# Packed queries, keys and queries of the first batches turned by TensorE; the second batch's expert chosen early; opening buffers and loads re-ordered

## The chip, the cores and the metric

One core of one Trainium2 chip runs the whole program. The metric is device time in microseconds, the median of several executions of the same program; smaller is better. TensorE multiplies matrices into eight PSUM banks, VectorE (DVE), ScalarE (ACT) and GpSimd (POOL) work on what it leaves, and SyncE (SP) issues nearly all DMA loads and stores, in the order of its program.

## What is computed

Shapes: 8 batches, 8 heads, 576 tokens, 64 values per head (model width 512), 32 packed queries per head, 8 experts with hidden width 1024. All data is float32.

```
p_packed = softmax(p @ k.T / 8) @ v           # 32 packed rows per batch and head
a        = softmax(q @ p_packed.T / 8) @ p_packed
x        = a with the heads side by side      # [8, 576, 512]
logits   = x @ w_gate ;  local = sigmoid(x @ w_local)
for each batch b, token s in order:
    fresh = argmax(logits[b, s])
    e     = fresh if s == 0 or local[b, s] < 0.5 else the expert of token s - 1
    out[b, s] = softmax(logits[b, s])[e] * (relu(x[b, s] @ w1[e]) @ w2[e])
```

## The kernel before

The kernel takes one expert per batch, that of token 0, and does all 576 tokens of the batch with it; a block behind the main program (L1170 on) repeats the batch for other experts if some token strayed. A batch's attention is done for two "quads" Q of four heads. Per quad: `scores` (L485) multiplies packed queries and keys, `keys` (L520 to L576) does the softmax, the product with v and turns the result to `ppT`; `queries` (L605) multiplies q with it, and `soften` (L642 to L668) turns the result to the softmax weights `a2t`, split into a rounded part `a2h` and a remainder `a2l`. x is never built: `pack_weights` (L932; in the first batch `pack_quarters`, L903) multiplies w1 with `ppT`, and `layer1` (L972) multiplies that with `a2h` and `a2l`. Each product is done as three (high times high, high times low, low times high), which is what the splits `wph`/`wpl` and `w2s` (L958, L960) are for. `layer2` (L1000, L1005, L1009) multiplies with w2 in 8 chunks, in two passes over the tokens ("half" 0 and 1).

**Who is turned where.** Scores need packed queries and keys with the 64 values on the partitions. In the first batch p was loaded four times (32 rows each, side by side on the partitions) and turned by DVE in blocks of 32 (L401), the keys too (L446, L448), so its score matmuls had 32 rows, and four DVE reductions per quad (L495) followed. Batch 1's keys and the queries of batches 0 and 1 were turned by TensorE in blocks of 128 (`turn_tokens`, L415 and L423, copied by ACT at L417 and L425); later batches are loaded in small blocks and turned by DVE (L439, L589).

**Who chooses the expert when.** `gates` (L759 to L843) takes logits of all tokens from the finished `a2t`. For the first batch alone, `early_choice` (L715 to L747) works out the logits of token 0 from its query (`q0`) and `ppT`; it holds one PSUM bank from its start to its choice. `choose` writes the expert's number, SP reads it into a register (`ereg`), and the loads of w1 (L869, L882) and w2 (L856) follow.

**What sets the order.** The program's order is made when it is built. Every step is a generator that yields conditions (`need`: tiles written, buffer slots and PSUM banks free, a condition `when`). `weave` (from L1133) takes the next step that is ready by a model of times (`Clock`), loads first, then side work of the earliest batch, then the main chunks; `soon` is the first batch without `ereg`, and later batches' side work waits for idle engines. Where the model sees TensorE wait, before the first chunks, it puts in matmuls on a constant tile (`keep_warm`, L214), one for each FILL ns. w1 and w2 of the first batch are loaded in the order `FIRST` ("1" a quarter of w1, "2" a chunk of w2, "v" the values of batch 1). Buffers per tag are in `BUFS`; `w2raw` has 4, `w2s` 8, `w1t` 2.

## Time and profile before

| what | value |
|---|---|
| median of 3 runs | 435.56 us (434.97 to 435.76) |
| profiled execution | 436.44 us, span 434.7 us |
| granted TensorE clock, mean | 0.987 |
| busy: TensorE, DVE, ACT, POOL | 416.2, 296.2, 177.6, 36.8 us |
| matmuls on the constant tile (L214) | 146 records, 22.2 us |
| one load of w1 (quarter), w2 (chunk), v (quad) | 512, 256, 512 KB |
| HBM read, written | 63.07 MB, 9.44 MB |

Busy shares are means over stages with different limits, so they are read stage by stage below. A float32 matmul leaves two records in the trace. A record's duration includes its way through the array, and matmuls overlap, so the duration of a group of them is the time that counts. L numbers are lines of the kernel before.

### The profile page before, as it was taken

The page shows a single profiled execution, that of the slowest core. Times are in us where ns is not written, and L with a number is a line of the kernel's source. Part 1 is how long each engine was busy: PE and PEld are TensorE (multiplying, and loading weights), DVE is VectorE, ACT ScalarE, POOL GpSimd, SP SyncE. Part 2 cuts the span into 40 slices and gives each one's busy share as a digit, 9 for nine tenths or more (in the row PEclk, how much of TensorE's full clock was granted, in tenths as well). Part 3 has the DMA queues.
Part 4 walks back from the last instruction along what each step waited for, and adds up shares of the span by engine and source line. Part 5 has one row for each costly group of instructions (what it writes and reads, how often), then busy time and mean ns, then how long its engine had stood idle before and what let it go on. Part 6 is the DMA issues. An engine that isn't in the chain of part 4 may idle for free.

```text
span 434.7 us, 10230 instructions
## 1 busy us (share of the span) xinstructions
PE 416.2 (96%) x3935; PEld 333.1 (77%) x3936; DVE 296.2 (68%) x862; ACT 177.6 (41%) x413; POOL 36.8 (8%) x56
## 2 busy tenths in 40 slices
PE   8899999959999999999999999999999999999994
PEld 8777787816887788786887588878887678878883
DVE  3576858677787588768967697829977588637221
ACT  1264743317342543435443462345433543345221
POOL 2001520200030000200020003000020000200000
PEclk9999999959999999999999999999999999999999
DMA  7879798074999379973999679983999340464011
GB/s 212 250 210 339 198 135 144 4 288 152 179 127 274 110 235 148 166 287 99 198 129 194 224 211 152 156 316 121 201 135 260 125 146 0 131 230 138 0 62 56
DMA packets 163024, 73.25 MB, mean 169 GB/s; under 512 B 127896, under 2 KB 143000, under 8 KB 162968
## 3 DMA queue, kind: packets, MB, share of 16 engines
q1 hardware_dynamic: 161720, 72.11, 74.7%
q8 instruction: 33, 0.54, 0.6%
q10 hardware_dynamic: 1248, 0.41, 0.4%
q14 instruction: 23, 0.19, 0.1%
HBM read 63.07 MB, written 9.44 MB: 167 GB/s over the span
## 4 chain that ended last, share of the span: by engine, by line
PE 80%; DVE 9%; DMA 4%; issue 3%; ACT 1%; SPq 1%; POOLq 0%; POOL 0%; DVEq 0%; ACTq 0%
PE bank L1000 36%; PE bank L972 20%; PE bank L1005 3%; PE bank L1009 3%; PE bank L214 3%; DMA w1t<-in_moe_w_dram 3%; PE bank L554 2%; PE bank L932 2%; PE bank L485 2%; PE bank L529 2%; DVE qn L589 2%; PE bank L605 2%; DMA qn<-in_q_dram 1%; DVE wpl L946 1%; DVE h L987 1%
## 5 line engine op out<-in xcount | busy, mean ns | idle before, releaser
L1000 PE MATMUL bank<-w2s,h 128*128 128x512 f32 x768 | 205.2, 399 | 2.3 <-DVE w2s L960 1.1
L1000 PEld LDWEIGHTS bank<-w2s,h 128*128 128x128 f32 x768 | 135.8, 188 | 32.7 <-issue 4.8
L987 DVE SCALAR_TENSOR_TENSOR h<-bank,h 128x256 fp32r<-128x256 f32 x192 | 61.1, 345 | 64.1 <-ACT h L983 63.9
L983 ACT ACTIVATE h<-bank 128x256 fp32r<-128x256 f32 (+1 forms) x128 | 52.9, 413 | 111.6 <-PE bank L972 107.0
L972 PEld LDWEIGHTS bank<-a2h,wph 128*128 128x128 f32 x256 | 47.0, 188 | 16.9 <-ACT wph L943 3.3
L972 PE MATMUL bank<-a2h,wph 128*128 128x320 f32 (+1 forms) x256 | 57.0, 304 | 0.0
L972 PE MATMUL bank<-a2h,wpl 128*128 128x320 f32 (+1 forms) x256 | 55.8, 297 | 1.0 <-DVE wpl L946 0.9
L972 PE MATMUL bank<-a2l,wph 128*128 128x320 f32 (+1 forms) x256 | 54.6, 294 | 0.0
L668 POOL TENSOR_TENSOR a2l<-a2t,a2h 128x576 fp32r<-128x576 f32 (+2 forms) x17 | 23.3, 1373 | 300.7 <-ACT a2h L665 300.7
L972 PEld LDWEIGHTS bank<-a2h,wpl 128*128 128x128 f32 x256 | 40.9, 188 | 2.0 <-DVE wpl L946 2.0
L972 PEld LDWEIGHTS bank<-a2l,wph 128*128 128x128 f32 x256 | 41.1, 188 | 0.0
L960 DVE TENSOR_TENSOR w2s<-w2raw,w2s 128x512 fp32r<-128x512 f32 x58 | 38.5, 693 | 0.6 <-ACT w2s L958 0.6
L958 ACT CAST w2s<-w2raw 128x512 fp32r<-128x512 f32 x64 | 38.0, 623 | 1.6 <-DMA w2raw<-in_moe_w_dram 1.4
L1005 PE MATMUL bank<-w2s,h 128*128 128x512 f32 x64 | 26.0, 406 | 0.0
L1009 PE MATMUL bank<-w2s,h 128*64 128x512 f32 x64 | 25.2, 394 | 0.0
L946 DVE TENSOR_TENSOR wpl<-bank,wph 128x512 fp32r<-128x512 f32 x28 | 18.1, 680 | 7.9 <-ACT wph L943 7.9
L214 PE MATMUL bank<-warm 128*128 128x128 f32 x146 | 22.2, 307 | 1.1 <-DVE warm L209 1.1
L214 PEld LDWEIGHTS bank<-warm 128*128 128x128 f32 x146 | 20.5, 219 | 1.8 <-issue 0.9
L520 ACT ACTIVATE a<-a,nb 128x576 f32<-128x576 f32 x16 | 12.4, 777 | 22.1 <-DVE nb L506 22.1
L943 ACT CAST wph<-bank 128x512 fp32r<-128x512 f32 x28 | 14.9, 599 | 11.8 <-PE bank L932 11.7
L625 DVE STREAM_TRANSPOSE sT<-bank 128x288 f32<-128x288 f32 (+2 forms) x36 | 13.2, 418 | 8.1 <-ACT gate L623 8.1
L495 DVE TENSOR_SCALAR_CACHE_REDUCE a<-bank 128x288 f32<-128x288 f32 (+2 forms) x36 | 13.6, 419 | 5.4 <-PE bank L485 5.1
(142 smaller groups left out, 445.2 us busy)
## 6 DMA issues: line engine op xcount, KB each, us to landing
w2raw<-in_moe_w_dram SPq DMA_DIRECT2D x64, 256.0 KB, 6.2
w1t<-in_moe_w_dram SPq DMA_DIRECT2D x14, 1024.0 KB, 6.1
kv<-in_v_dram SPq DMA_DIRECT2D x16, 512.0 KB, 6.1
out_dram<-o SPq DMA_DIRECT2D x31, 256.0 KB, 2.1
qn<-in_k_dram SPq DMA_DIRECT2D x24, 288.0 KB, 7.3
qn<-in_q_dram SPq DMA_DIRECT2D x24, 288.0 KB, 6.9
kv<-in_q_dram SPq DMA_DIRECT2D x4, 512.0 KB, 6.6
w1t<-in_moe_w_dram SPq DMA_DIRECT2D x4, 512.0 KB, 5.5
```

What stands on the lines that cost most here:

```text
L214: nc.tensor.matmul(out=warm_ps[:, :128], lhsT=warm, rhs=warm, start=True, stop=True)
L668: eng.tensor_tensor(out=a2l, in0=a2t, in1=a2h.bitcast(F32), op=ALU.subtract)
L943: nc.scalar.copy(out=hi[fh][:, Q], in_=ts[fh, Q])
L946: nc.vector.tensor_tensor(out=lo[fh][:, Q], in0=ts[fh, Q], in1=hi[fh][:, Q].bitcast(F32), op=ALU.subtract)
L958: nc.scalar.copy(out=w[:, 0], in_=raw)
L960: (nc.gpsimd if st["early"] and c > 1 else nc.vector).tensor_tensor(out=w[:, 1], in0=raw, in1=w[:, 0].bitcast(F32), op=ALU.subtract)
L972: nc.tensor.matmul(out=t[:, :GROUP * (m1 - m0)], lhsT=st["wp"][c // 4][wi][:, Q, fs], rhs=a2[ai][Q][:, GROUP * m0:GROUP * m1], start=(n == ...
L983: nc.scalar.activation(out=h[:, :w], in_=t[:, :w], func=AF.Relu)
L987: nc.vector.scalar_tensor_tensor(out=h[:, dst:dst + z - a], in0=t[:, a:z], scalar=0.0, in1=h[:, a:z].bitcast(F32), op0=ALU.max, op1=ALU.su ...
L1000: nc.tensor.matmul(out=acc, lhsT=hs[hi], rhs=w[:, wi], start=(c == 0 and n == 0), stop=(c == NC - 1 and n == 2),)
L1005: nc.tensor.matmul(out=acc, lhsT=h[:, 256:WIDE + TAIL], rhs=w[:, 0], start=(c == 0), stop=False, skip_group_check=True,)
L1009: nc.tensor.matmul(out=acc[0:TAIL], lhsT=h[:, 256:WIDE], rhs=w[:, 1], start=False, stop=(c == NC - 1), skip_group_check=True,)
```

## The change

Packed queries are loaded once, 128 rows (four heads by 32) by two groups, twice side by side on the free axis, and turned by two TensorE transposes and one ACT copy; this holds for batches 0 and 1. Batch 0's keys go the way of batch 1's: `turn_tokens`. Its score matmuls have 64 rows, so two reductions per quad follow. Keys and queries of the first two batches are loaded into other slots (`w2s`, `kv`, and `o` for the last 64 tokens). Batch 1 gets `early_choice` and `gate_weights`, with a second `q0`. Its queries are loaded from `FIRST`, behind the first w1 pieces, and its remainders of w2 are subtracted by POOL. The constant matmuls are bf16 of 512 columns instead of float32 of 128; the model doubles TensorE's times up to 6500 ns and starts it at 3700 instead of 5400. `soon` and some conditions ask for `settled` (expert known and softmax done) instead of `ereg`.

```
-WARM, FILL = 10, 240.0
+WARM, FILL = 6, 230.0
-START, FIRST_LOAD = 5400.0, 700.0
+START, FIRST_LOAD, COLD = 3700.0, 700.0, 6500.0
-FIRST = "1 2 1 2 2 v 1 2 1 2 2 2 2".split()
+FIRST = "1 2 1 2 2 q 1 2 v 1 2 2 2 2".split()
...
+            full *= 2.0 if self.engine("PE") < COLD else 1.0
...
-            nc.tensor.matmul(out=warm_ps[:, :128], lhsT=warm, rhs=warm, start=True, stop=True)
+            nc.tensor.matmul(out=warm_ps, lhsT=heat[:, :128], rhs=heat, start=True, stop=True)
...
+    def settled(b):
+        return "ereg" in sts[b] and sts[b]["quads"] == [NQ, NQ]
...
     def load_packs(b, queues):
-        x = tile_([128, H, D], F32, "p_in")
-        clock.rate = 150.0
+        x = tile_([128, 2, 2 * D], F32, "p_in")
+        clock.rate = 400.0
         for z, queue in enumerate(queues):
-            queue.dma_start(out=x[NP * z:NP * z + NP], in_=at(p, b).rearrange("h n d -> n h d"))
+            queue.dma_start(out=x[:, :, D * z:D * z + D], in_=at(p, b).rearrange("(g h) n d -> (h n) g d", g=2))
...
-            st["p"] = load_packs(b, (nc.sync, nc.scalar, nc.sync, nc.scalar))
+            st["px"] = load_packs(b, (nc.sync, nc.scalar))
...
-            order = (("k", 0), ("k", 1), ("q", 0), ("q", 1), ("p", 1)) if st["second"] else \
+            order = (("k", 0), ("k", 1), ("p", 1)) if st["second"] else \
...
+            if name == "q" and isinstance(b, int) and b == 2:
+                yield need(when=lambda: len(sts[1].get("w1", ())) == 2)
...
     def turn_packs(st):
-        yield need(when=lambda: "p" in st)
-        yield need(st["p"])
-        turn(st["p"])
-        st["pT"] = st["p"].rearrange("a h (x n) -> a h x n", n=NP)
+        yield need(when=lambda: "px" in st)
+        yield need(st["px"], slot="pT", banks=1, by=("Activation",))
+        tp = bank()
+        for g in range(2):
+            nc.tensor.transpose(out=tp[:, 128 * g:128 * g + 128], in_=st["px"][:, g], identity=ident)
+        give(st["px"])
+        yield need(tp, by=("Activation",))
+        st["p"] = st["pT"] = tile_([128, H * NP], F32, "pT")
+        nc.scalar.copy(out=st["pT"], in_=tp[:, 0:H * NP])
+        give(tp)
...
-                nc.scalar.copy(
+                (nc.vector.tensor_copy if early and Q == 0 and n else nc.scalar.copy)(
...
-        if part is None:
+        if part is None and not st["pairs"]:
...
-            if not st["early"]:
+            if not st["pairs"]:
                 yield from choose(st, cd[0:1, 0:1])
...
-                        yield need(slot="kv")
-                        sts[1]["v", Q] = load_values(1, Q)
+                        yield need(slot="kv" if kind == "v" else ("kv", "o"))
+                        sts[1][kind, Q] = load_values(1, Q) if kind == "v" else load_pairs(sts[1], kind, Q)
...
-            (nc.gpsimd if st["early"] and c > 1 else nc.vector).tensor_tensor(
+            (nc.gpsimd if st["second"] or st["early"] and c > 1 else nc.vector).tensor_tensor(
...
-                    *((turn_packs(st), early_choice(st), turn_small()) if early else ()),
-                    *((turn_tokens(st, "k"), turn_keys(st, 0)) if started == 1 else (turn_keys(st, Q) for Q in both)),
+                    *((turn_small(),) if early else ()), *((early_choice(st),) if started < 2 else ()),
+                    *((turn_packs(st), turn_tokens(st, "k")) if started < 2 else (turn_keys(st, Q) for Q in both)),
...
-            soon = next((b for b in range(B) if "ereg" not in sts[b]), B) if at_batch[0] >= 0 else 0
+            soon = next((b for b in range(B) if not settled(b)), B) if at_batch[0] >= 0 else 0
```

## Rows read from the trace of the kernel before

**Rows 1.** Stretches: us; busy us of PE, PEld, DVE, ACT, POOL; clock, DMA, GB/s.

```profile
1.00:7.00 6.00, 5.90 (x27) 5.91 (x28) 2.87 (x8) 1.28 (x1) 2.00 (x11) 1.00 0.76 203
34.50:43.20 8.70, 7.79 (x75) 6.11 (x74) 5.74 (x16) 2.89 (x8) 1.29 (x1) 1.00 1.10 335
43.20:86.60 43.40, 43.37 (x458) 34.61 (x458) 30.41 (x108) 20.50 (x53) 11.81 (x13) 1.00 0.71 122
86.60:99.45 12.85, 7.47 (x70) 2.13 (x70) 9.14 (x29) 3.02 (x7) 0.00 (x0) 0.60 0.68 246
99.45:426.00 326.55, 322.73 (x2839) 260.26 (x2831) 231.14 (x634) 136.79 (x312) 20.30 (x24) 1.00 0.77 163
```

**Rows 2.** Chain of waits in order of time: start, us, what.

```profile
1.10 8.45 PE bank L214 x48
...
10.73 2.43 PE bank L214 x20
...
35.42 7.68 DMA w1t<-in_moe_w_dram
```

**Rows 3.** Timeline of the opening: start, us, engine, line, operation.

```profile
6.24 0.43 DVE L448 STREAM_TRANSPOSE kf<-kf 64x256 f32<-64x256 f32 x1
...
9.48 1.12 PE L485 MATMUL bank<-kf,p_in 32*32 32x160 f32 x64
...
11.60 1.23 DVE L446 STREAM_TRANSPOSE kf<-kf 128x1024 f32<-128x1024 f32 x1
...
22.09 0.27 ACT L576 COPY ppT<-bank 128x128 f32<-128x128 f32 x1 [2.03 <-PE bank L575]
...
34.53 0.54 PE L972 MATMUL bank<-a2h,wph 128*128 128x320 f32 x2
```

**Rows 4.** Timeline of SP's queue, 20 to 140 us: issues of loads.

```profile
27.72 0.42 SPq L869 DMA_DIRECT2D w1t<-in_moe_w_dram  x1
...
38.62 8.53 SPq L856 DMA_DIRECT2D w2raw<-in_moe_w_dram  x4
...
52.45 7.93 SPq L336 DMA_DIRECT2D qn<-in_k_dram  x4
...
85.56 1.08 SPq L882 DMA_DIRECT2D w1t<-in_moe_w_dram  x2
```

**Rows 5.** Timeline of PE: w1 packed for batch 1 and for batch 2.

```profile
96.04 3.48 PE L932 MATMUL bank<-w1t,ppT 64*32 64x512 f32 x32
...
143.88 1.95 PE L932 MATMUL bank<-w1t,ppT 64*32 64x512 f32 x32
```

**Rows 6.** Timeline of PE and DVE: prices of single steps.

```profile
10.49 0.32 DVE L495 TENSOR_SCALAR_CACHE_REDUCE a<-bank 128x160 f32<-128x160 f32 x1 [3.82 <-PE bank L485]
...
19.42 0.27 PE L715 MATMUL bank<-q,ppT 64*32 64x32 f32 x8
...
21.18 0.66 PE L415 MATMUL bank<-ident,kv 128*128 128x128 f32 x4
...
46.32 1.20 PE L485 MATMUL bank<-qn,p_in 64*32 64x288 f32 x32
...
47.07 0.46 DVE L495 TENSOR_SCALAR_CACHE_REDUCE a<-bank 128x288 f32<-128x288 f32 x1
...
61.74 0.29 PE L554 MATMUL bank<-v_rest,a_rest 128*32 128x64 f32 x8
```

**Rows 7.** Timeline of DVE and POOL, 49 to 83 us.

```profile
49.80 2.72 POOL L960 TENSOR_TENSOR w2s<-w2raw,w2s 128x512 fp32r<-128x512 f32 x2 [1.59 <-ACT w2s L958]
...
50.15 1.22 DVE L656 TENSOR_TENSOR sT<-sT,sm 128x256 f32<-128x256 f32 x1
...
52.82 0.43 DVE L656 TENSOR_TENSOR sT<-sT,sm 128x256 f32<-128x256 f32 x1
...
81.40 1.42 POOL L668 TENSOR_TENSOR a2l<-a2t,a2h 128x576 fp32r<-128x576 f32 x1 [1.24 <-ACT a2h L665]
```

**Rows 8.** Costliest groups: xcount, busy us, mean ns, idle before.

```profile
L987 DVE SCALAR_TENSOR_TENSOR h<-bank,h 128x256 fp32r<-128x256 f32 x192 | 61.1, 345 | 64.1 <-ACT h L983 63.9
```

More of the change, by code (lines that the diff above doesn't have):

```diff
@@ L403, in turn_tokens @@
     def turn_tokens(st, name):
-        yield need(slot="qn", when=lambda: (name, 0) in st and ("a2t" in st if st["early"] else sts[0]["asked"] >= NQ))
+        early = st["early"] and name == "k"
+        yield need(slot="qn", when=lambda: (name, 0) in st and (early or ("a2t" in st if st["early"] else sts[0]["asked"] >= NQ)))
         xT = st[name] = tile_([128, NQ, HQ, HALF], F32, "qn")
@@ L451, in turn_keys @@
-        if Q == 0 and not st["early"]:
+        yield need(when=lambda: "k" in st and "p" in st and (not isinstance(st["b"], int) or "ereg" in sts[st["b"] - 1]))
+        yield need(st["k"])
+        kT = st["k"].rearrange("a (h q) x -> a q h x", q=NQ)[:, Q]
+        nc.vector.transpose(out=kT, in_=kT)
+        st["kT", Q] = kT
+        if Q == 0:
             yield need(st["p"])
             turn(st["p"])
-            st["pT"] = st["p"].rearrange("a h (x n) -> a h x n", n=NP)
+            st["pT"] = st["p"].rearrange("a h n -> a (h n)")
@@ L464, in scores @@
+        st["p"] = st["pT"] = tile_([128, H * NP], F32, "pT")
+        nc.scalar.copy(out=st["pT"], in_=tp[:, 0:H * NP])
+        give(tp)
     def scores(st, Qs):
-        yield need(when=lambda: "pT" in st and all(("kT", Q) in st for Q in Qs) and (not st["second"] or "begun" in sts[0]))
+        yield need(when=lambda: "pT" in st and all(("kT", Q) in st for Q in Qs))
         yield need(slot=(("a1", len(Qs)),))
-        n = 4 if st["early"] else 2
         sc = {Q: tile_([128, SPAD], F32, "a1") for Q in Qs}
-        m4 = {Q: tile_([128, 4], F32, "m4") for Q in Qs}
@@ L472, in parts @@
-        def parts(x, r):
-            if n == 4:
-                return x.rearrange("a (c r i) -> a c r i", c=NJ + 1, r=4)[:, 0:NJ + (r < 2), r]
-            return x[:, 0:S].rearrange("a (m r) -> a r m", r=2)[:, r]
-        yield need(st["p"], *(y for Q in Qs for y in ((st["kT", Q],) if st["second"] else (st["k", Q],) if st["early"] else (st["k"],))), banks=n * len(Qs))
-        ts = {(Q, r): bank() for Q in Qs for r in range(n)}
-        steps, rows = (2, NP) if st["early"] else (1, 2 * NP)
@@ L479, in scores @@
-        for Q in Qs:
-            for x in range(steps):
-                for r in range(n):
-                    ps_ = slice(rows * r, rows * r + rows)
-                    cs = NJ + (r < 2)
-                    for h in range(HQ):
-                        nc.tensor.matmul(
-                            out=ts[Q, r][32 * h:32 * h + 32, :32 * cs if n == 4 else HALF],
-                            lhsT=st["pT"][ps_, NQ * h + Q, x],
-                            rhs=st["kT", Q][ps_, h, x, 0:cs] if st["early"] else st["kT", Q][ps_, h],
-                            start=(x == 0), stop=(x == steps - 1),
-                        )
+        m2 = {Q: tile_([128, 2], F32, "m2") for Q in Qs}
@@ new lines, in scores @@
+        yield need(st["p"], *(st["kT", Q] if st["pairs"] else st["k"] for Q in Qs), banks=2 * len(Qs))
+        ts = {(Q, r): bank() for Q in Qs for r in range(2)}
+        for Q in Qs:
+            for r in range(2):
+                ps_ = slice(64 * r, 64 * r + 64)
+                for h in range(HQ):
+                    nc.tensor.matmul(
+                        out=ts[Q, r][32 * h:32 * h + 32, :HALF],
+                        lhsT=st["pT"][ps_, NP * (NQ * h + Q):NP * (NQ * h + Q) + NP],
+                        rhs=st["kT", Q][ps_, h],
+                        start=True, stop=True,
+                    )
@@ L621, in queries @@
         for Q in Qs:
-            if part is None:
+            if part is None and not st["pairs"]:
                 nc.scalar.copy(out=st["gate"][:, Q, 0:GW], in_=ts[Q, 0][:, HALF:HALF + GW])
@@ L681, in gate_weights @@
     def gate_weights(st):
-        yield need(when=lambda: None not in st["ppT"] and "small" in st)
+        yield need(when=lambda: None not in st["ppT"] and "small" in sts[0])
         yield need(*st["ppT"], wgl, banks=1)
@@ L711, in early_choice @@
         for Q in range(NQ):
-            yield need(when=lambda: st["ppT"][Q] is not None and "small" in st)
-            yield need(st["ppT"][Q], q0)
+            yield need(when=lambda: st["ppT"][Q] is not None and "small" in sts[0])
+            yield need(st["ppT"][Q], q0[st["b"]])
             for h in range(HQ):
@@ L959, in splits @@
             yield need(w)
-            (nc.gpsimd if st["early"] and c > 1 else nc.vector).tensor_tensor(out=w[:, 1], in0=raw, in1=w[:, 0].bitcast(F32), op=ALU.subtract)
+            (nc.gpsimd if st["second"] or st["early"] and c > 1 else nc.vector).tensor_tensor(out=w[:, 1], in0=raw, in1=w[:, 0].bitcast(F32), op=ALU.subtract)
             give(raw)
```

133 lines of the change are left out of this document (56 added, 77 removed), and 2 rows, old and new, of the table BUFS.

## The prediction

> **What bounds the kernel now.** I read the stages first. From 43.20 to 86.60 us TensorE is busy 43.37 of 43.40 us, and from 99.45 to 426.00 us 322.73 of 326.55 us [rows 1]: there the kernel is bound by TensorE, and only fewer matmuls would help. Three stretches are not like that: the opening, the 8.70 us after it, and 86.60 to 99.45 us, where TensorE is busy 7.47 of 12.85 us at a granted clock of 0.60.
>
> The chain of waits shows what fills the opening: warm-up matmuls that do no work, 8.45 us at the start and 2.43 us between the first real steps, with smaller ones behind [rows 2]. They stand in TensorE's program, so what comes behind them waits even when its data is there. The timeline shows that it was: the last transpose of the first quad's keys starts at 6.24 us, and the first score matmul at 9.48 [rows 3]. The chain then runs over the packed values (ppT copied at 22.09), the expert's choice and the first w1 load at 27.72 to the first expert matmul at 34.53 [rows 3, 4]. After that DMA is the limit: its share is 1.10 at 335 GB/s [rows 1], and the third w1 quarter costs 7.68 us of waiting [rows 2].
>
> The gap at 86.60 is one wait. SyncE issues batch 1's w1 at 85.56 [rows 4], because batch 1's expert is chosen only from its finished softmax. By then the first batch has 1 us of work left before 86.60. TensorE fills the gap with batch 2's scores and transposes and with the packing of w1 (L932, 3.48 us against 1.95 us at the next transition) [rows 5].
>
> **The change part by part.** *Gap before batch 1.* early_choice for batch 1 needs ppT and the gate weights, not the softmax. Its values matmul ends at 62.03 [rows 6]; from ppT to the first w1 the first batch took 27.72 - 22.09 = 5.6 us [rows 3, 4], so batch 1's w1 could be asked for by about 70, and SP is then past the key blocks that it issues from 52.45 for 7.93 us [rows 4]. So it is issued some 15 us before 85.56 and w1 is there when the first batch ends. What must still run of the 12.85 us is one batch of scores (1.20), five transposes (0.66 for four) and one packing (1.95) [rows 5, 6]: about 4.0 us, with overlaps 3.6. At best 9.3 us go. Batch 2, which has its weights in time, packs without a wait before it [rows 5], so the best case is near; for relu, copies and a second w1 half that lands late I leave 0.7: **-8.6** (ends -5.5 and -9.3). The next late thing is batch 1's a2l, last made on POOL at 81.40 + 1.42 = 82.82 [rows 7]; that is 3.8 us before 86.60, and a shift of the opening moves both.
>
> *Opening.* Packs come once instead of four times (128 KB for 256), so keys land about 128/250 = 0.5 us earlier, and the warm-ups end sooner. Keys are there at 6.24 at the latest [rows 3], so now at 5.7. The transposes go to TensorE: four cost 0.66 us [rows 6], in the first 7 us about twice that, as 27 records in 5.90 us there [rows 1] against 20 in 2.43 [rows 2] show although the clock's row reads 1.00. Most hide under the loads; behind the last load stand one transpose and a copy, about 1.0 us with waits. Scores at 6.8 instead of 9.48 is **-2.6**. Scores of a quad are half of the 1.20 us of two [rows 6], so no slower than 1.12 [rows 3]; two reductions (2 x 0.46) replace four (4 x 0.32) [rows 6]: **-0.3**. Behind that, the second quad's keys were turned by DVE at 11.60, behind the first quad's reductions [rows 3]; on TensorE and ACT they run beside them, and the fill of 2.43 [rows 2] and those behind it may shrink. That is worth 0 to 3.6 us; I take 1.6, under half, because the fill is still planned against guessed times: **-1.6**. Together -4.5; ends +1 (ACT's copies come onto the path, nothing else is won) and -6.5.
>
> From the choice to the first expert matmul nothing is counted. Before the third w1 quarter stand the same 3.4 MB as before, queries in the place of values, so the DMA-bound stretch moves as a whole; the fourth quarter waits for 1.2 MB of values more, 3.5 us at 335 GB/s, and lands about when it is needed. 0, ends -1 and +2.
>
> *TensorE's new work between 43.20 and 86.60*, where nothing hides it: the choice's matmuls (two groups of 0.27, and one like them behind), gate weights by themselves (no dearer than what they replace), two pack transposes (half of 0.66) [rows 6]: **+1.1**, ends 0.7 and 1.5. Changes of tile shape are in these rows.
>
> *Batch 1's w2 split on POOL.* Eight subtractions leave DVE for POOL (2.72 us for two) [rows 7]. In the first batch six such (c > 1 in L960) stood beside a full TensorE [rows 1], so I take **+0.5**, ends 0 and 4. The row to watch: DVE's L656 took 1.22 us at 50.15 while POOL worked from 49.80 to 52.52, and 0.43 us at 52.82 after it [rows 7]. The softmax of batch 1 is next to the new POOL work.
> By the Trainium skill (SBUF — State Buffer, Who interferes with whom) a VectorE instruction with two SBUF inputs and a GpSimd instruction that reads SBUF lock each other out for a whole instruction. These two rows agree (0.43 becomes 1.22). It speaks against this edit, and its outcome is the third rival.
>
> *One PSUM bank.* Batch 1's early_choice takes a bank as soon as one is free and keeps it until its choice. The trace has no row for a TensorE short of a bank; sixteen chunks that each waited for one L987 (345 ns on average [rows 8]) would lose 5.5 us: ends 0 and 5.5; I take 0, because batch 0's choice held a bank too.
>
> **Sum.** The profiled execution took 436.44 us (span 434.7). -8.6 -2.6 -0.3 -1.6 +1.1 +0.5 = -11.5, so 424.9; the median of the runs, 435.56, is 0.88 below the profiled one: **424.1 us**.
>
> **Rivals.**
> 1. *The opening wins nothing.* Fills or DMA take it back; for it, DMA at 1.10 from 34.50; against it, keys that lay ready from 6.24 to 9.48. 424.1 + 4.5 = 428.6.
> 2. *The gap moves one batch on.* Once batch 1's expert is known, batch 2's loads wait until all of batch 1's w2 is issued. If that holds up keys and not only queries, batch 2's expert is late and the 9 us stand at the next transition: 424.1 + 8.6 = 432.7. Against it, batch 2's keys went out at 52.45 [rows 4], well before the choice could be known.
> 3. *POOL holds up batch 1's a2l.* If all eight splits (8 x 1.36 = 10.9) come before it, it is ready at 93.7 instead of 82.8, 7 us behind 86.60, and 6 of the gain go: 430. The splits can only start when the first batch gives back its w2s buffers, one per chunk, so about half is likely.
> 4. *The other side: SP stands at the register read.* SP works in order, and the read of batch 1's expert waits there. If it is queued ahead of the first batch's last four w2 loads (38.62 on [rows 4]), they come only after a choice at some 60 us. That is 60 - 4.5 - 38.6 = some 17 us later than now, and the first batch stalls for them: 424.1 + 17 = 441. It decides from 12 us of waiting on. Against it: batch 1's values are themselves queued among these loads, and the choice needs them.
>
> **How the numbers follow.** Forecast 0.60, first rival 0.16, second 0.08, third 0.07, fourth 0.07; 0.02 that the choice comes no earlier for the loads and only the opening counts (about 433). About 0.2% is what a measurement can tell from no change. All but the fourth are faster; I leave 0.02 for "same": faster 0.90, same 0.02, slower 0.08. The forecast's own range, from the ends of its large terms, is 419 to 428.5. To hold 8 in 10 it must reach over the first and third rivals, and some way to the second: 418 to 432.
>
> **What would show it.** Right: first score matmul near 7 us; first expert matmul near 30; w1 of batch 1 issued before 75; no granted clock below 1.00 between the first batch and the second; L932 there at 1.95 us. Wrong: a gap of more than 3 us on TensorE at the first or the second transition, L960 on POOL ahead of L668 with DVE's L656 above 1 us, or SyncE silent between 40 and 60 us.

## The result, and the profile after

The kernel after takes **430.46 us** (median of 4 runs, 429.87 to 432.28) against 435.58 before on the same chip: ratio **0.989, 95% interval 0.986 to 0.992**. The forecast was 424.1, so 5.1 us were won of 11.5. The profiled execution took 430.42 us, span 428.6 (before: 436.44 and 434.7). Line numbers of after are 14 below those of before for most of TensorE's work: L986, L958, L918, L477 are before's L1000, L972, L932, L485; L946 is L960, L973 is L987.

To see where the time went, the run is cut at marks that both kernels have: the first expert product (L958), and for each batch the first product L991 (before: L1005), which in these two kernels stands some 5 us behind the batch's first expert product and is called its **start** here. The starts of batches, in us:

| kernel | first L958 | 1 | 2 | 3 | 4 | 7 |
|---|---|---|---|---|---|---|
| before | 34.5 | 104.7 | 154.9 | 203.1 | 254.6 | 393.2 |
| after | 33.3 | 92.3 | 146.5 | 196.1 | 245.2 | 387.0 |

The stretches between them, of before: first expert product to batch 1's start, batch 1's pass, batch 2's start to batch 7's. Columns: us; busy us of PE, PEld, DVE, ACT, POOL; clock, DMA, GB/s.

```profile
34.50:104.70 70.20, 63.56 (x626) 46.91 (x625) 49.75 (x161) 31.50 (x79) 13.10 (x14) 0.93 0.73 173
104.70:154.90 50.20, 49.90 (x532) 40.13 (x531) 36.54 (x105) 21.76 (x52) 3.71 (x4) 1.00 0.90 172
154.90:393.20 238.30, 235.09 (x2098) 187.81 (x2097) 177.34 (x490) 100.94 (x231) 16.59 (x20) 1.00 0.83 176
```

The same stretches of after:

```profile
33.30:92.30 59.00, 58.55 (x601) 44.00 (x600) 43.22 (x140) 28.62 (x70) 14.04 (x14) 1.00 0.86 206
92.30:146.50 54.20, 52.02 (x568) 40.88 (x567) 43.43 (x134) 24.69 (x60) 12.76 (x13) 1.00 0.95 188
146.50:387.00 240.50, 235.65 (x2100) 187.69 (x2099) 175.96 (x487) 102.44 (x232) 16.41 (x20) 1.00 0.78 172
```

Batch 1 starts 12.4 us sooner, and the slow clock of the first stretch (0.93) is gone. But batch 1's own pass takes 54.2 us for 50.2: TensorE stands idle for 2.2 us of it and does 2.1 us of work more, since what had run in the old gap now runs here. And the passes from batch 2 to batch 7, for which the change touches only conditions of the order (`settled`), take 2.2 us more.

**The opening.** Timeline of after (start, us, engine, line; in brackets the idle time before it and what ended it):

```profile
6.32 0.69 DVE L424 COPY qn<-bank 128x512 f32<-128x512 f32 x1 [4.03 <-PE bank L422]
...
9.16 0.99 PE L422 MATMUL bank<-ident,kw 128*128 128x128 f32 x4 [2.12 <-DMA kw<-in_k_dram]
10.09 1.21 PE L477 MATMUL bank<-qn,pT 64*32 64x288 f32 x16
...
23.84 0.41 PE L458 MATMUL bank<-ident,p_in 128*128 128x128 f32 x2 [0.88 <-DMA p_in<-in_p_dram]
24.17 0.31 PE L723 MATMUL bank<-gate,et 128*32 128x32 f32 x4
...
26.33 0.40 SPq L855 DMA_DIRECT2D w1t<-in_moe_w_dram  x1
...
33.26 0.54 PE L958 MATMUL bank<-a2h,wph 128*128 128x320 f32 x2
```

The first quad's keys are turned and copied at 7.01 us (6.32 + 0.69), as forecast. The scores (L477) start at 10.09 all the same: TensorE works in order, and ahead of them its program has the transposes of the second quad's keys, which wait for their load until 9.16. Later the choice (L723) stands behind the transposes of batch 1's packs (L458), whose load comes at 23.84. Stretches of the opening, columns as above:

```profile
8.00:10.00 2.00, 0.84 (x4) 0.60 (x4) 0.00 (x0) 0.00 (x0) 0.00 (x0) 0.83 1.13 283
10.00:12.00 2.00, 2.00 (x21) 1.00 (x21) 0.67 (x3) 0.63 (x1) 0.00 (x0) 0.50 1.12 279
12.00:14.00 2.00, 2.00 (x23) 0.82 (x21) 0.34 (x3) 1.54 (x4) 0.00 (x0) 0.81 0.93 273
```

**The transitions.** Timeline of after, batch 2's keys, the choices and the packing of w1:

```profile
62.83 7.82 SPq L340 DMA_DIRECT2D qn<-in_k_dram  x4
...
73.80 1.01 SPq L868 DMA_DIRECT2D w1t<-in_moe_w_dram  x2
...
85.08 1.95 PE L918 MATMUL bank<-w1t,ppT 64*32 64x512 f32 x32
...
125.19 0.65 PE L745 MATMUL bank<-a2t,gate 128*32 128x128 f32 x16
...
128.50 1.01 SPq L868 DMA_DIRECT2D w1t<-in_moe_w_dram  x2
...
136.31 0.74 PE L515 MATMUL bank<-ident,a 128*128 128x128 f32 x4 [2.03 <-ACT a L506]
...
137.09 1.95 PE L918 MATMUL bank<-w1t,ppT 64*32 64x512 f32 x32
...
146.53 0.47 PE L991 MATMUL bank<-w2s,h 128*128 128x512 f32 x1
```

Batch 1's w1 goes out at 73.80 instead of 85.56 [rows 4], and its packing (85.08) takes 1.95 us instead of 3.48 [rows 5]. Batch 2 is now the late one: its gates (L745) stand at 125.19, its w1 goes out at 128.50, TensorE waits, and it starts at 146.53, 21.3 us after its gates. The row puts the wait of 2.03 us down to batch 3's softmax (L506), which TensorE's order has ahead of the packing; when batch 2's w1 landed, the profile does not show.

### The profile page after: what moved, and what is told of

Its sections match the earlier page's. It is cut to its first block, busy times and chain, and to the rows that moved or that the text cites. A ratio compares the mean times of both kernels' runs of the same rounds, so it can differ in the third digit from the quotient of the medians.

```text
span 428.6 us, 9926 instructions
## 1 busy us (share of the span) xinstructions
PE 410.8 (96%) x3784; PEld 320.0 (75%) x3785; DVE 292.4 (68%) x853; ACT 180.8 (42%) x420; POOL 46.8 (11%) x65
## 4 chain that ended last, share of the span: by engine, by line
PE 76%; DVE 8%; SPq 5%; DMA 5%; issue 2%; ACT 2%; POOLq 0%; POOL 0%; DVEq 0%; ACTq 0%
PE bank L986 37%; PE bank L958 21%; PE bank L991 4%; PE bank L995 3%; PE bank L540 2%; PE bank L918 2%; DVE wpl L932 2%; PE bank L591 2%; PE bank L515 2%; PE bank L477 2%; DMA kv<-in_q_dram 1%; DMA qn<-in_q_dram 1%; SPq L324 1%; DVE qn L575 1%; DVE h L973 1%
## 5 line engine op out<-in xcount | busy, mean ns | idle before, releaser
L986 PE MATMUL bank<-w2s,h 128*128 128x512 f32 x768 | 207.4, 400 | 4.6 <-DVE w2s L946 3.1
L986 PEld LDWEIGHTS bank<-w2s,h 128*128 128x128 f32 x768 | 135.4, 188 | 35.6 <-issue 5.2
L973 DVE SCALAR_TENSOR_TENSOR h<-bank,h 128x256 fp32r<-128x256 f32 x192 | 61.5, 348 | 58.6 <-ACT h L969 58.3
L958 PEld LDWEIGHTS bank<-a2h,wph 128*128 128x128 f32 x256 | 47.0, 188 | 17.4 <-ACT wph L929 2.3
L958 PE MATMUL bank<-a2h,wph 128*128 128x320 f32 (+1 forms) x256 | 56.9, 302 | 0.3
L958 PE MATMUL bank<-a2h,wpl 128*128 128x320 f32 (+1 forms) x256 | 55.9, 298 | 0.1
L958 PE MATMUL bank<-a2l,wph 128*128 128x320 f32 (+1 forms) x256 | 54.6, 294 | 0.0
L958 PEld LDWEIGHTS bank<-a2h,wpl 128*128 128x128 f32 x256 | 41.0, 188 | 1.0 <-DVE wpl L932 1.0
L958 PEld LDWEIGHTS bank<-a2l,wph 128*128 128x128 f32 x256 | 41.0, 188 | 0.0
L946 DVE TENSOR_TENSOR w2s<-w2raw,w2s 128x512 fp32r<-128x512 f32 x50 | 32.4, 683 | 0.8 <-ACT w2s L944 0.7
L991 PE MATMUL bank<-w2s,h 128*128 128x512 f32 x64 | 26.0, 406 | 0.0
L932 DVE TENSOR_TENSOR wpl<-bank,wph 128x512 fp32r<-128x512 f32 x28 | 18.3, 683 | 6.8 <-ACT wph L929 6.8
L946 POOL TENSOR_TENSOR w2s<-w2raw,w2s 128x512 fp32r<-128x512 f32 x14 | 17.9, 1300 | 27.4 <-ACT w2s L944 22.6
L929 ACT CAST wph<-bank 128x512 fp32r<-128x512 f32 x28 | 14.8, 599 | 11.5 <-PE bank L918 11.5
L485 DVE TENSOR_SCALAR_CACHE_REDUCE a<-bank 128x288 f32<-128x288 f32 x32 | 13.3, 454 | 8.7 <-PE bank L477 8.2
L651 ACT CAST a2h<-a2t 128x576 fp32r<-128x576 f32 (+2 forms) x18 | 11.1, 625 | 13.2 <-DVE a2t L645 10.3
L575 DVE STREAM_TRANSPOSE qn<-qn 128x1152 f32<-128x1152 f32 x12 | 16.5, 1373 | 0.1
```

The source lines that it names most:

```text
L575: nc.vector.transpose(out=qT, in_=qT)
L929: nc.scalar.copy(out=hi[fh][:, Q], in_=ts[fh, Q])
L932: nc.vector.tensor_tensor(out=lo[fh][:, Q], in0=ts[fh, Q], in1=hi[fh][:, Q].bitcast(F32), op=ALU.subtract)
L946: (nc.gpsimd if st["second"] or st["early"] and c > 1 else nc.vector).tensor_tensor(out=w[:, 1], in0=raw, in1=w[:, 0].bitcast(F32), op=ALU ...
L958: nc.tensor.matmul(out=t[:, :GROUP * (m1 - m0)], lhsT=st["wp"][c // 4][wi][:, Q, fs], rhs=a2[ai][Q][:, GROUP * m0:GROUP * m1], start=(n == ...
L973: nc.vector.scalar_tensor_tensor(out=h[:, dst:dst + z - a], in0=t[:, a:z], scalar=0.0, in1=h[:, a:z].bitcast(F32), op0=ALU.max, op1=ALU.su ...
```

## The experiments

Times are medians with the ratio to before. All kernels keep to after's text but for the edits shown (cut at `...`); their lines differ from after's by a few. The marks are those of one profiled execution each; d1's took 438.6 us and e1's 441.6, 4.2 and 2.0 more than their medians.

Among kernels with after's own opening (after, a4, b1, b2, c1, c3, e1, e2, f1, f2) the first L958 stands between 32.8 and 36.3 us, although up to there TensorE's instructions come in the same order in all of them (some records of the constant matmuls apart). So these 3.5 us are the spread of single executions, not the work of the edits, and a smaller difference in the first L958 shows nothing. In the eight kernels whose opening is edited as a2's or a3's it stands between 29.3 and 30.6, outside that spread.

| kernel | us | ratio (95%) | first L958 | start 1 | 2 | 3 | 7 |
|---|---|---|---|---|---|---|---|
| after | 430.5 | 0.989 (0.986-0.992) | 33.3 | 92.3 | 146.5 | 196.1 | 387.0 |
| a1 | 430.8 | 0.989 (0.985-0.993) | 32.8 | 92.1 | 146.3 | 195.7 | 386.6 |
| a2 | 433.7 | 0.996 (0.993-1.000) | 30.1 | 95.5 | 149.8 | 199.1 | 389.6 |
| a3 | 432.6 | 0.992 (0.989-0.995) | 29.9 | 94.8 | 149.1 | 198.4 | 389.0 |
| a4 | 438.9 | 1.006 (1.003-1.009) | 33.0 | 104.6 | 155.8 | 204.8 | 395.0 |
| b1 | 437.2 | 1.004 (1.001-1.006) | 32.8 | 107.1 | 156.0 | 205.4 | 393.3 |
| b2 | 435.6 | 1.001 (0.999-1.003) | 34.5 | 95.7 | 152.8 | 202.2 | 392.8 |
| b5 | 430.5 | 0.989 (0.987-0.991) | 29.8 | 90.5 | 146.4 | 195.8 | 386.2 |
| b6 | 434.7 | 0.997 (0.995-0.999) | 29.3 | 89.5 | 151.2 | 200.4 | 390.7 |
| c1 | 428.6 | 0.982 (0.979-0.986) | 34.8 | 93.8 | 144.3 | 195.5 | 386.2 |
| c2 | 434.4 | 0.995 (0.993-0.998) | 30.2 | 90.0 | 138.2 | 199.9 | 390.5 |
| c3 | 430.6 | 0.988 (0.984-0.991) | 33.0 | 93.8 | 148.5 | 197.8 | 388.3 |
| c4 | 431.8 | 0.990 (0.986-0.994) | 29.3 | 89.6 | 137.8 | 198.1 | 388.9 |
| d1 | 434.4 | 0.995 (0.993-0.997) | 30.6 | 94.0 | 142.1 | 196.1 | 395.4 |
| d2 | 442.8 | 1.017 (1.013-1.020) | 29.5 | 88.8 | 137.0 | 190.0 | 398.9 |
| e1 | 439.6 | 1.008 (1.005-1.011) | 36.3 | 96.2 | 158.2 | 207.5 | 398.1 |
| e2 | 434.3 | 0.996 (0.994-0.997) | 34.3 | 93.4 | 147.6 | 199.3 | 390.0 |
| f1 | 427.2 | 0.981 (0.977-0.985) | 34.1 | 93.2 | 148.4 | 195.8 | 384.1 |
| f2 | 429.2 | 0.986 (0.982-0.989) | 34.0 | 93.2 | 143.6 | 195.1 | 385.7 |

**The opening: a1, a2, a3.** a1 takes the second quad's keys from ahead of the first scores, a2 batch 1's packs from ahead of the first choice, a3 both.

```diff
 # a1, in turn_tokens
-(early or st["second"] or ...)
+(early and (Q == 0 or st["scored"] > 0) or st["second"] or ...)
 # a2, in turn_packs
-yield need(when=lambda: "px" in st)
+yield need(when=lambda: "px" in st and (st["early"] or "ereg" in sts[0]))
```

> Changed kernel, with the second quad's keys (first batch) turned only after the first quad's scores. Theory A: in the changed kernel TensorE, in order, stood at 9.16 us for the load of the second quad's keys, and the first quad's scores (keys copied by 7.01) were queued behind it until 10.09; so the scores start near 7.3, the clock stays at 1.00 in 8 to 12 us, and ppT of the second quad is done near 18.5 instead of 20.36. The choice still waits for batch 1's packs (landed 23.7, transposed ahead of the choice's last matmul), so the time falls by 0 to 1 us only. Rival: the second quad's keys land at 9.1 and set ppT anyway; scores start early, ppT moves by less than 0.7 us, and the time is the same.

> Changed kernel, with batch 1's packs turned only after the first batch's choice. Theory A: the transposes of batch 1's packs, waiting for their load until 23.7, held the choice's matmul (L723) and with it w1; w1 goes out at 25.4 instead of 26.33, the first expert matmul comes 0.5 to 0.9 us earlier, and so does the end. Rival: the first batch's softmax on DVE and ACT sets the first expert matmul; w1 goes out earlier and the time is the same.

> Both edits. Theory A: they uncover each other: scores near 7.3, w1 out near 23.5, first expert matmul near 30.5 instead of 33.26, and the end 2 to 3 us earlier, as the opening's term of the prediction had it. Rival (the opening is bound by DMA or by DVE behind the scores): less than 1 us.

a3's first scores start at 7.7 us and its first expert product at 29.9: -4.6 against before, the -4.5 of the forecast. Most of that comes with a2 (30.1); a1's first scores start at 7.9, but its first expert product comes only 0.5 us sooner, less than the spread named above. None of the three makes the kernel faster than after. In a2 and a3 batch 1 starts 3.2 and 2.5 us later than in after. Timeline of a2, POOL and TensorE before batch 1:

```profile
84.84 2.51 POOL L946 TENSOR_TENSOR w2s<-w2raw,w2s 128x512 fp32r<-128x512 f32 x2 [0.78 <-ACT w2s L944]
87.31 1.40 POOL L654 TENSOR_TENSOR a2l<-a2t,a2h 128x576 fp32r<-128x576 f32 x1
...
88.76 0.63 PE L958 MATMUL bank<-a2l,wph 128*128 128x320 f32 x1 [2.30 <-POOL a2l L654]
...
89.72 2.76 PE L986 MATMUL bank<-w2s,h 128*128 128x512 f32 x6
```

The first batch is done sooner, its w2s buffers come free, batch 1's w2 splits go ahead of its a2l on POOL, and TensorE waits for a2l: the third rival, by its mechanism, in a kernel whose opening is as fast as forecast. The wait costs twice: behind it the clock is 0.50 from 88 to 94 us, and the six products at 89.72 take 2.76 us, where after's at 88.64 took 1.56. From batch 1's first product to its start it takes 10.5 us instead of 4.6.

**That mended: b5, b6.** b5 is a3 with batch 1's packing of w1 held until batch 1 is settled (its expert chosen and its softmax done); b6 has its w2 remainders on DVE besides.

```diff
 # in pack_weights
-yield need(when=lambda: len(st.get("w1", ())) > fhs[-1])
+yield need(when=lambda: len(st.get("w1", ())) > fhs[-1] and (not st["second"] or settled(1)))
```

> Both edits of the opening (second quad's keys behind the scores, batch 1's packs behind the choice), and batch 1's w1 packed only when its softmax is done. Theory D: in the kernel with both edits the opening won 3.4 us against the changed kernel, but batch 1 began later, because in the order of the program DVE's remainders of the packed w1 (L932) stood ahead of the last softmax transposes (83.07) and POOL's w2 remainders ahead of a2l (86.72). With the softmax first, a2l is done by 84, batch 1's first L991 comes near 90 instead of 94.8, and the total is 427 to 429. Rival: the packing, now behind the softmax, opens a gap of its own before batch 1 (L918, ACT's and DVE's copies: 5 us), and the total stays near 432.

> The same with batch 1's w2 remainders on DVE. Theory D: one POOL remainder is still queued ahead of the last a2l, and DVE is blocked by the others; without them a2l comes 1 us earlier and the total is up to 1.5 us below the kernel with the remainders on POOL. Rival: the 0.69 us pieces on DVE delay batch 1's first chunks and batch 2's chain by as much; the same or 1 to 2 us more.

In b5 both early gains stand: first product 29.8, batch 1 at 90.5. Yet batch 2 starts at 146.4, as in after, and the time is after's. The opening's 3.5 us are won and lost again within 120 us. b6, expected to gain up to 1.5 us more, loses 4.2: with the splits on DVE batch 2 starts at 151.3.

**The parts undone: b1, b2.** b1 leaves out the early choice of batch 1 (and the wait of batch 2's queries for its w1); b2 puts batch 1's w2 remainders back on DVE.

```diff
 # b2, in splits
-(nc.gpsimd if st["second"] or st["early"] and c > 1 else nc.vector).tensor_tensor(...)
+(nc.gpsimd if st["early"] and c > 1 else nc.vector).tensor_tensor(...)
```

> Changed kernel without its early choice for batch 1: batch 1 chooses from its finished softmax again, and batch 2's queries no longer wait for its w1. Theory B: the early choice closes the gap before batch 1 and nothing else in the change does; so the gap is back (batch 1's w1 out near 84, its packing near 95) while the opening stays 1.3 us ahead: total 434 to 435, and batch 1's pass falls from 54.2 to about 50, because batch 2's scores run in the gap again. Rival: batch 1's start is set by its softmax in any case; it moves by less than 4 us and the total by less than 2.

> Changed kernel with batch 1's eight w2 remainders on DVE instead of POOL. Theory C: on POOL they block DVE instructions with two SBUF inputs (L772 took 1.13 instead of 0.20, L824 1.20) and stand in batch 2's way; on DVE batch 2's chain is not slower, and the total is the same or up to 1 us less. Rival (the prediction's term had +0.5 for POOL): DVE is the tighter engine in batch 1's pass; 8 x 0.69 us more there makes batch 2's expert later, and the total rises by 1 to 3 us.

Without either part nothing is left of the gain (1.004 and 1.001). From the first expert product to batch 2's start it takes 123.2 us without the early choice (107.1 - 32.8 to batch 1, then 48.9), 118.3 without POOL's splits, 113.2 with both, 120.4 before. The splits on POOL, costed at +0.5, are worth 5.1 us there, but only behind the early choice: without it they leave the stretch longer than before's. TensorE's waits in b2 at the two transitions:

```profile
94.46 1.42 PE L986 MATMUL bank<-w2s,h 128*128 128x512 f32 x5 [1.83 <-DVE w2s L946]
...
141.56 1.13 PE L515 MATMUL bank<-ident,a 128*128 128x128 f32 x4 [2.99 <-ACT a L506]
142.84 2.71 PE L918 MATMUL bank<-w1t,ppT 64*32 64x512 f32 x32
```

Of the 5.1 us, 2.2 lie ahead of batch 1's start, where b2 waits 1.83 us for a split on DVE; 0.7 lie between that start and batch 2's gates; the rest lies behind these gates, where the wait is 2.99 us instead of 2.03 and the packing takes 2.71 instead of 1.95, at a clock of 0.66 between 141 and 146.

**What holds batch 2: a4, e1, e2, c3.** a4 lets the side work for batch 2 go as soon as batch 1's expert is known. e1 turns batch 2's keys three times instead of once (the keys are the same), 4 x 1.37 = 5.5 us of DVE's time; e2 does so at batch 4. c3 moves the scaling of two output blocks of batches 0 to 2 from DVE to ACT.

```diff
 # a4, in weave: the first batch that is not settled
-soon = next((b for b in range(B) if not settled(b)), B) ...
+soon = next((b for b in range(B) if not (settled(b) or b == 1 and "ereg" in sts[1])), B) ...
 # e1 (e2: == 4), in turn_keys
-nc.vector.transpose(out=kT, in_=kT)
+for _ in range(3 if isinstance(st["b"], int) and st["b"] == 2 else 1):
+    nc.vector.transpose(out=kT, in_=kT)
 # c3, in store
+if isinstance(b, int) and b < 3:
+    nc.scalar.activation(out=o, in_=acc, func=AF.Copy, scale=pe[:, i:i + 1])
```

> Changed kernel; batch 2's side work is let in as soon as batch 1's expert is known, not only when its softmax is done. Theory B: batch 1's pass became 5 us longer (51.4 instead of 46.4) because batch 2's scores, which ran in the old gap, now come 5 us into batch 1's pass and make batch 2's expert late (w1 out at 128.5, batch 1's work done at 133.1). With the scores some 8 us earlier w1 of batch 2 goes out near 121, the gap before batch 2 goes, and the time falls by 2.5 to 3.5 us. Rival: DVE is full from 70 to 82 us with batch 1's softmax; what is put in there pushes batch 1's a2l behind the end of the first batch, a gap opens before batch 1, and the time is the same or longer.

> The kernel after, with batch 2's keys turned three times by VectorE instead of once (turning twice more gives the same keys back): 4 x 1.37 = 5.5 us more of VectorE's work after batch 1's gates and before batch 2's scores. If batch 2's start hangs on its attention chain, which begins when batch 1's ends (gates 83.5, scores 92.9, gates 125.2, start 146.5), then batch 2's gates come 4 to 5.5 us later (129 to 131) and it starts at 150.5 to 152, while batch 1 starts near 92.3 to 94; the time is 434 to 436. If the chain has slack there and TensorE's work alone sets the start, it stays at 146.5 and the time within 1 us of 430.5.

> The same 5.5 us of VectorE's work at batch 4's keys instead of batch 2's. If the chain of attention is late only for the first batches and has caught up by batch 4 (its gates at 215.9 stand 29 us ahead of its start at 245.2, where batch 2 has 21), the time stays within 1 us of 430.5. If VectorE is as tight in every pass, this costs as much as at batch 2: 3 to 5.5 us.

> The kernel after, with the scaling of the second and third output blocks (0.74 us each on VectorE, 128x512) on ScalarE for batches 0 to 2; these are two instructions in each pass, 1.5 us of VectorE's time. If VectorE is what sets batch 1's gates and batch 2's start (theory B), batch 2 starts about 1.5 us sooner, near 145, and the time is about 429. If batch 2's start hangs on the place of its choice and not on VectorE's load (theory A), or on ScalarE, the starts stay at 92.3 and 146.5 and the time within 0.7 us of 430.5.

In a4 batch 2's scores move from 92.9 to 81.2 us, but batch 1's gates from 83.5 to 93.1, and batch 1 starts 12.3 us later: side work for batch 2 is paid by batch 1.

e1 lengthens batch 1's pass from 54.2 to 61.9 us. Batch 2's gates stand 38.4 us behind batch 1's start instead of 32.9, later by all of the 5.5 us put in. But the transposes also hold up TensorE directly, since h, the output of the first layer, stands behind them in DVE's order. The waits in e1 and in e2 (their L987 is after's L986):

```profile
101.26 0.50 PE L987 MATMUL bank<-w2s,h 128*128 128x512 f32 x1 [3.05 <-DVE h L974]
...
177.99 2.08 PE L987 MATMUL bank<-w2s,h 128*128 128x512 f32 x4 [2.96 <-DVE h L974]
```

In e2 this wait is the whole loss of its pass: the pass in which it stands, batch 2's, takes 51.7 us for 49.6, and batch 4 then starts 28.5 us behind its gates, where after has 29.3. So at batch 4 the chain had slack. e2's time is 3.8 us above after's all the same, which the expectation had for a chain as tight as at batch 2; 1.1 of them are there at the first L958.

So the start of batch 2 hangs on its chain of attention on DVE, ACT and TensorE, which begins when batch 1's has ended, and later chains have slack. Taking 1.5 us of DVE's work out of the pass (c3) changes nothing: 54.8 us for 54.2. That points to what stands in the chain rather than to DVE's sum of work, but does not settle it: the same edit in c4 is worth 2.6 us beside c2 (below), 0.9 of them at the first L958.

**Batch 2 chosen early as well, and more: c1, c2, d1, d2.** c1 is after with the early choice for batch 2 (its query 0 in the small load, its gate weights made apart, its PSUM bank taken once both ppT are there). c2 is b5 with the same, c4 is c2 with c3's edit (where the expectations of c2 and c4 say that batch 1's packing is kept behind batch 0, the edit is b5's, behind batch 1's own softmax); d1 adds batch 3 to c2, d2 all batches (their queries 0 wait in one small tile).

```diff
 # c1 and c2 (d1: < 4, d2: < 8)
+st["ahead"] = isinstance(b, int) and b < 3
-*((early_choice(st),) if started < 2 else ()),
+*((early_choice(st),) if started < 3 else ()),
-*((gate_weights(st),) if started < 2 else ()), gates(st),
+*((gate_weights(st),) if started < 3 else ()), gates(st),
```

> The kernel after, with the early choice for batch 2 as well: its query 0 comes with the small load, its expert is chosen as soon as its pixel matrices stand, and its gate weights are made as those of batches 0 and 1 are. Theory A: batch 2's start is set by its own choice, which stands at the end of its attention chain (gates 125.2, w1 issued 128.50, packs 137 to 139). Then w1 of batch 2 goes out before 115, the 2.9 us in which TensorE is idle between 130 and 139.6 go, batch 2's first product of the fourth block moves from 146.5 to about 143, and the time is about 427.5 if the later passes keep their lengths. Theory B: VectorE, full through batch 1's pass, sets it: the gate weights still stand behind the same work, batch 2 starts at 146 or later, and the time is 430 to 432, since the early choice adds VectorE's work for one more batch. Theory C: batch 2 starts sooner but batch 3 gives it back, as batch 1 did in the kernel after: start of batch 2 near 143, start of batch 3 at 196 as now, time 430.

> The kernel with the opening's keys and packs moved behind the first scores and batch 1's packed weights kept behind batch 0's settling, which started batch 1 at 90.5 and batch 2 at 146.4, with the early choice for batch 2 added. Theory A (batch 2's late choice took the gain back): batch 1 still starts near 90.5, batch 2 near 141.5, and the time is about 425.5, near the forecast of the change. Theory B (VectorE sets batch 2's start): batch 2 at 146 to 147 and 430.5. Theory C (given back at batch 3): batch 2 near 142, batch 3 at 196, time 430.

> The opening's order, batch 1's packed weights behind batch 0's settling, the early choice for batch 2, and the scaling of two output blocks of batches 0 to 2 on ScalarE, all together. Theory A: as without the scaling moved, about 425.5. Theory B: the relief of VectorE is what counts: 1.5 us or more below the same kernel with the scaling on VectorE, batch 2's start sooner by as much. Theory C: batch 3 at 196 as now and 430, whatever the first three batches do.

> The kernel with the opening's new order, batch 1's packed weights behind batch 0's settling and early choices for batches 0 to 2 (starts of batches 1, 2, 3 at 90.0, 138.2, 199.9), with the early choice for batch 3 as well. Theory A (the gap stands wherever the choice is the first late one: start = gates + 21 us where a batch is chosen at the end of its attention chain, gates + 7 where it was chosen early): batch 3's gates stand near 174.6 as they did, so it starts at 187 to 189 instead of 199.9, batch 4 at 238 to 240, and the time is 424 to 426, the forecast. Theory B (each early choice itself costs the attention chain: gates of batch 2 came at 131.4 with it and 124.0 without): the chain falls further behind, batch 4 becomes the late one, starts at about 249, and the time is again near 434.

> The same with every batch's expert chosen early. Theory A: no batch has a late choice, batches 1 to 7 start at 90, 138 and then every 49 us, so batch 7 starts near 383 and the time is 424 to 425. Theory B: the attention chain, with one more choice in each batch, sets the pace: passes of over 50 us and 432 or more.

c1, batch 1's pass (columns as above):

```profile
93.80:144.30 50.50, 50.45 (x502) 39.17 (x501) 40.49 (x125) 22.41 (x53) 12.50 (x13) 1.00 0.94 194
```

The idle time of 2.2 us is gone and the pass takes 50.5 us. So the late choice did set batch 2's start. In c2 batch 2 starts at 138.2, 8.3 us before after, but its gates come at 131.4, where b5, the same kernel without this choice, has 124.0. Then the gap is at batch 3, whose w1 goes out at 177.83:

```profile
175.00:180.00 5.00, 4.03 (x42) 3.10 (x34) 3.60 (x13) 0.82 (x4) 0.79 (x3) 1.00 0.19 28
180.00:185.00 5.00, 2.13 (x32) 0.57 (x32) 4.93 (x17) 0.67 (x1) 0.00 (x0) 0.69 1.05 398
185.00:190.00 5.00, 3.37 (x18) 2.01 (x26) 2.53 (x15) 2.44 (x8) 0.00 (x0) 0.50 0.55 204
```

TensorE is idle for 5.5 of these 15 us, the clock falls to 0.50, and batch 3 starts at 199.9 (198.1 in c4, whose DVE has less to do). My theory for d1 and d2 was that the gap stands wherever the first late choice is; it fell: in d1 batch 3 starts at 196.1 us, not at 187 to 189, and batch 4 at 252.9 (245.2 in after). With every choice early (d2) passes of 48 to 55 us follow one another: the gates of batches 1 to 4 stand at 82.5, 130.3, 179.6 and 232.9, the first two steps 47.8 and 49.3 us, where after has 41.7 and 41.2 (83.5, 125.2, 166.4). TensorE's groups in d2, from batch 2's start to batch 7's (columns: count, busy us, mean ns, idle before them and what ended most of it):

```profile
L965 PE MATMUL bank<-a2l,wph 128*128 128x320 f32 (+1 forms) x160 | 36.7, 306 | 3.5 <-POOL a2l L658 3.4
...
L752 PE MATMUL bank<-a2t,gate 128*32 128x128 f32 x80 | 4.2, 295 | 7.6 <-DVE a2t L649 7.6
```

TensorE waits for the softmax itself (a2t, a2l), no longer for weights, and DVE is busy 199 of 262 us. These waits are not all: of the 21.4 us by which the stretch is longer than after's, 6.6 are idle time and 14.8 TensorE's own. A pass has some 464 records for 420, since the choice and its gate weights are work of their own, and the clock is 0.94 to 0.97 in three of the five passes.

So an early choice slows the chain of attention. Two reasons are likely, and no run separates them: its steps run between those of the chain, and the weights that it brings in early are packed and split on the same engines.

**POOL once more: f1, f2.** Batch 2's w2 remainders on POOL too, in after (f1) and in c1 (f2).

```diff
 # in splits
-(nc.gpsimd if st["second"] or st["early"] and c > 1 else nc.vector).tensor_tensor(...)
+(nc.gpsimd if isinstance(st["b"], int) and (st["b"] in (1, 2) or st["b"] == 0 and c > 1) else nc.vector).tensor_tensor(...)
```

> The kernel after, with batch 2's w2 remainders on POOL as batch 1's are (eight subtractions of 0.68 us each leave VectorE, all of them after batch 2's w1 goes out at 128.5). Batch 2's own chain of attention is over by then (gates 125.2), so its start should stay at 146.5; if VectorE's weight work is what slows the chain, batch 3's gates come some 3 to 5 us sooner than 166.4, which have slack, and the time stays within 1 us of 430.5. Rival: the subtractions on POOL hold up the first products of batch 2, as POOL's 1.36 us for one is twice VectorE's 0.68: start 148 to 150, time 432 to 434.

> The kernel after with the early choice for batch 2 (starts 93.8, 144.3, 195.5) and batch 2's w2 remainders on POOL. They now fall between 122 and 145, where batch 2's gates (129.0) and batch 3's scores (132.7) are. If VectorE's load is what pushes the chain back after an early choice (theory B), the relief of 5.5 us gives batch 3's gates at 165 to 168 instead of 169.8, a start of batch 3 near 193.5, and a time of 426 to 427. If the chain is held by the order of its steps and not by VectorE's load, nothing moves: 428.6 within 1 us. Rival: POOL's work ahead of batch 2's a2l, or beside VectorE's two-input instructions, costs 2 to 4 us: 431 or more.

f1 has the lowest time, 427.2 us (its interval overlaps c1's), against the expectation of no change: batches 1 and 2 start no sooner, but batch 2's start to batch 7's takes 235.7 us instead of 240.5. The group of second-layer products shows it, of after between these starts:

```profile
L986 PE MATMUL bank<-w2s,h 128*128 128x512 f32 x481 | 130.7, 401 | 4.3 <-DVE w2s L946 3.1 <-DVE h L973 0.9
```

and of f1:

```profile
L986 PE MATMUL bank<-w2s,h 128*128 128x512 f32 x481 | 129.2, 399 | 0.0
```

In after TensorE waits about 1 us in three of the later batches for its first w2 split on DVE; in f1 never, though those batches' splits are on DVE in both: the packing of w1 stands 15.9 us ahead of batch 6's start in f1 (325.2 to 341.1), 8.5 in after (334.9 to 343.4). Why relief at batch 2 keeps the lead to the end was not taken apart. f2 gives c1's time within its interval: there the wait is still 3.6 us.

## Why the prediction was wrong

Its sum was -11.5 us on the profiled execution; the span fell by 6.1. (Two of its terms are rounded down: 9.48 - 6.8 is 2.7, and 1.28 - 0.92 is 0.36.) By the marks:

| stretch | forecast | measured |
|---|---|---|
| to the first expert product | -2.6 -0.3 -1.6 = -4.5 | -1.3 (34.53 to 33.26) |
| from there to batch 2's start | -8.6 +1.1 +0.5 = -7.0 | -7.2 (120.4 to 113.2) |
| batch 2's start to batch 7's | 0 | +2.2 (238.3 to 240.5) |

By medians 5.1 us were won; the other 0.9 is that the profiled execution of before lay above its median and that of after does not. The -1.3 is less than the 3.5 us by which single executions differ there.

*Opening, the step that failed first.* "Behind the last load stand one transpose and a copy", so "Scores at 6.8": the copy was done at 7.01, but the scores were at 10.09, because in TensorE's order the next quad's transposes, with a load still under way, came ahead of them. I had counted the first quad's way and left out what is queued in front. The same held at the choice, behind batch 1's packs. Once these two are put behind (a3), the three terms together come to their -4.5 (-4.6), partly by luck: the scores give -1.8 for -2.6, and what follows 2.8 for 1.9.

*Opening, what it is worth.* The sum took it as a gain to the end. a3 and b5 show that it is not: with 29.9 and 29.8 at the first product, batch 2 comes no sooner. Putting the opening right would not have saved the forecast. In b5 batch 1's gates stand at 84.1 as against 83.5, although the opening is 3.5 us shorter. The first rival (428.6, the opening wins nothing) is what happened in effect; its reason, fills or DMA, is half the matter: what takes the gain back are steps that wait for loads and that TensorE's order puts too far in front. The third rival's price (430) lies nearer to the 430.5, by chance: in after POOL starts the last a2l at 82.65 and batch 1's first split only at 88.86.

*Gap before batch 1.* Every sign of this term came: w1 out at 73.80, packing at 1.95 us, the clock at 1.00 from 73.80 to 92.30. From the first expert product batch 1 starts after 59.0 us for 70.2, -11.2, more than the -8.6; 2.2 of that are POOL's (61.2 in b2). What failed is the next sentence: "Batch 2, which has its weights in time, packs without a wait before it". It had them in time because the gap gave it time. Its gates stood at 127.5 and moved only to 125.2, while batch 1 moved by 12.4, and 21.3 us later it started. The trace of before gave a warning: 127.5 plus 20.5, the shortest way from gates to start there (batch 7, 372.7 to 393.2), is 148.0, and the sum needed 143.4 (154.9 - 11.5). It is the second rival in its effect (the gap moved on, 4.0 us of it), not in its mechanism: batch 2's keys were not held up, they went out at 62.83 and DVE turned the first of them at 82.33; and releasing batch 2's side work sooner (a4) made it worse.

*POOL's splits.* Costed at +0.5, with the lock-out of DVE as the danger. Without them the gain is gone (b2): they save 5.1 us, most of it in TensorE's waits at the two transitions and 0.7 in the chain of attention between. So the -7.2 agrees with -7.0 by two errors that cancel: without POOL's 5.1 only 2.1 us of the gap's 7.5 (8.6 less 1.1) would be left. The danger is real, but small in after. Timeline of DVE and POOL there:

```profile
103.39 5.03 POOL L946 TENSOR_TENSOR w2s<-w2raw,w2s 128x512 fp32r<-128x512 f32 x4 [7.05 <-ACT w2s L944]
...
105.04 0.92 DVE L821 TENSOR_SCALAR fresh_all<-gz 128x5 f32<-128x5 f32 x1
...
106.00 1.20 DVE L824 TENSOR_TENSOR pe<-pe,gsm 128x5 f32<-128x5 f32 x1
```

L824 takes 1.20 us beside POOL and 0.16 in the median of its 8 instances. That agrees with the Trainium skill (SBUF — State Buffer, Who interferes with whom): a VectorE instruction with two SBUF inputs contends with a GpSimd instruction that reads SBUF.

*Later passes.* Their term was put at nothing, since "there the kernel is bound by TensorE, and only fewer matmuls would help". They took 2.2 us more, and in f1, without fewer matmuls there, 2.6 us less than before. TensorE's idle time in them was 3.2 us before, 4.9 in after and 1.6 in f1, by waits of about 1 us a batch that a busy share of 98% hides. So 1.6 of the 2.2 us are such waits; why after has more of them than before stays open.

*Register read.* The fourth rival did not come. SP did stand still between 46.2 and 59.6 us, one of the signs named, but all eight w2 loads of the first batch were out by 44.6, and what it issued next were batch 2's values.

## What to carry to other kernels

A gap in which the bounding engine waits is also time in which the others get ahead. Before counting it as won, work out for the next two items when their own chain ends and how long after it they can start; an item starts at the later of the two times, its own and that of the gap's end. On an engine that works in order, the time at which an operation's data is there says nothing until what is queued ahead of it is listed with the time of its data. Work moved to an idle engine is to be priced by the waits that it takes away on the engine it leaves, not only by what it may disturb. And a mark of one execution is to be compared only with the spread of that mark among executions in which nothing ahead of it was changed.

## What the runs showed of the hardware that was not expected

In the opening of after TensorE was idle for 2.12 us until 9.16; the clock was 0.83 between 8 and 10 us and 0.50, the lower of its two levels, between 10 and 12. The 16 score matmuls at 10.09 took 1.21 us there and 0.72 us at 45.16. In a2 idle times of 0.47 and 2.30 us before 88.76 were followed by 0.50 from 88 to 94. In the gap of c2, with 5.5 idle us in 15, the clock was 0.50 between 185 and 190. But the 2.03 idle us until 136.31 in after left it at 1.00 from 134 to 139.

A VectorE instruction with a single tensor input, too, took longer beside POOL's splits: L821 took 0.92 us at 105.04 in after, and 0.16 in the median of its 8 instances; L807 took 1.28 us at 95.86 in b5, and 0.16 in the median. That POOL's reads held them up is inferred from the overlap in time.
